# Infini-attention and Hedgehog attention in one kernel: the memory update from f16 halves of the key features, turned by a DMA, and a reordered plan

## The chip, the cores and the metric

The kernel runs on one core of a Trainium2 chip. A core has five engines with an instruction queue each: TensorE (PE in the profile; its weight loads are PEld), VectorE (DVE), ScalarE (ACT), GpSimd (POOL) and SyncE (SP), which here only issues DMAs. The metric is the time of one launch on the device in microseconds, as the median over runs.

## The reference, cut to what matters

Two attention layers on 2048 tokens, width 1024, 32 heads of 32; the results stand side by side in the output.

Part A is attention in four segments of 512 tokens with a memory M and its normaliser z for each head:

```python
phi = lambda t: jnp.where(t > 0, t + 1.0, jnp.exp(t))
for s in range(N):                     # N = 4 segments
    a_dot = softmax(qs @ ks.T * scale + mask) @ vs
    pq = phi(qs)
    num = jnp.einsum("bhld,bhde->bhle", pq, M)
    den = jnp.einsum("bhld,bhd->bhl", pq, z)[..., None] + 1e-6
    outs.append(g * num / den + (1.0 - g) * a_dot)
    pk = phi(ks)
    M = M + jnp.einsum("bhld,bhle->bhde", pk, vs)
    z = z + jnp.einsum("bhld->bhd", pk)
```

Part B is linear attention: per head a feature map (two softmaxes) of a learned projection of queries and keys, sums of key features times values over all tokens, then a quotient for each query. Both parts end in an output product with a 1024 x 1024 matrix.

## The kernel before, in words

**Number format.** Nearly all products take float32 values as two f16 halves (high, and the rest as low) and add three f16 products: high-high, high-low, low-high. ACT makes the high half as a copy with a scale, DVE or POOL the low half by a subtraction. Some products are still in float32; each of those is two records of the trace.

**The plan.** The program records every step as an operation with an engine, an expected duration, a priority and its dependencies (`Graph.op`). `Graph.run` then walks through expected time: whenever an engine is free, it takes the ready operation with the smallest priority (ties by order of recording) and emits it. That fixes the order in every engine's queue, and each queue is worked off in that order. It also hands out the eight PSUM banks by kind ("proj", "s", "misc", "pv", "kv", with limits for each; at most three "proj" at a time). Where it expects PE to wait for more than 0.5 us, `Graph.fill` emits float32 products of an identity matrix with itself into a free bank ("fill"), which keep PE active.

**Part A's units.** A unit is one segment `s` and one group `g` of four heads; 32 units, priority 2u. The first half takes segments 0 and 1 for all groups, the second segments 2 and 3. `produce(u)` projects keys (m = 1), then queries (m = 0), 24 f16 products of 512 columns each, and makes from PSUM the f16 halves of both (`h3`) and the features (`pk` unless the segment is the last, `pq` unless it is the first). SP copies the halves into `st` in the layout that scores need. `values(u)` projects values with 96 products of 128 columns; ACT writes them scaled in float32 to `vf` (three buffers, with a column of ones for each of the four heads). `attend(u)` finds row maxima (L796 products, L802 on DVE), makes the halves `vl` of the values from `vf` (L835 on ACT, L837 on DVE; two buffers), reads the memory (L849), updates it, and does scores (L894), exponential and halves (L898, L900, L901), causal masks on POOL (L907), head products (L930), and writes its result to DRAM.

**The memory update before.** For each of the 24 units whose segment is not the last: `pk` is relu(k) + exp(-relu(-k)), from two Relu steps and an exponential on ACT and an addition on POOL. In `attend`, four float32 transposes on PE turn it (L864), ACT copies the result from PSUM to `pkt` (L626), four float32 products with `vf` give the update (L869), DVE multiplies it with the mask `bdm` (the gate on each head's block, and head columns for z; L872), and POOL adds it to `mem` (L873).

**Around it.** While part A runs, other work is mixed into the queues by priority: loading and splitting of weights and segments; `fold`, which multiplies part B's weights with its feature map; halves of part B's value weights and of two pairs of its token tiles. Then the key stage of part B (`strassen`, feature softmax `expo`, sums L1294 from the halves `pt` of L1284 and L1287), the query stage with the output product of part B (L378 misc), and the output product of part A (L1539). The query stage already turns f16 tiles of 128 x 1024 with a DMA issued by SP (L1467).

**Segment loads.** `load_seg(s)` fetches a segment in two pieces of 1 MB, takes the largest magnitude and makes halves. Segments 0 and 1 have their own slots for both pieces. Segments 2 and 3 share one slot, S11, so the first piece is fetched again after the second was used.

Of the kernel before, what the change touches and what calls it, by code (L numbers as in the profile page):

```python
# [8 lines left out]
F32 = mybir.dt.float32  # L9
# [9 lines left out]
S = 2048  # L19
# [24 lines left out]
EUP = 2.0 ** 15  # L44

# [17 lines left out]
class Op:  # L63
    __slots__ = ("eng", "dur", "fn", "prio", "lat", "deps", "wait", "ready", "short", "port", "banks", "place", "known", "safe", "kb")


class Graph:
# [36 lines left out]
    def op(self, eng, dur, fn, r=(), w=(), prio=0, lat=0.0, short=False, port=False, need=(), kb=256):  # L104
        o = Op()
        o.short, o.port = short, port or eng == "POOL"
        o.eng, o.dur, o.fn, o.prio, o.lat, o.kb = eng, dur, fn, (prio, len(self.ops)), lat, kb
        o.banks = []
        ends, starts = set(), set()
        for b in need:  # L110
            if b.prev[0] is not None:
                ends.update(b.prev[0].ops)
        for write, accs in ((0, r), (1, w)):
            for acc in accs:
                b, key = acc if isinstance(acc, tuple) else (acc, None)
# [24 lines left out]
        self.ops.append(o)  # L140
        return o
# [120 lines left out]
def tile_kernel(ctx: ExitStack, tc: tile.TileContext, ax, aw, awv, awo, beta, bx, bwqk, bwv, bphi, bwo, out):  # L262
# [57 lines left out]
    bdm = ca.tile([128, NG, 132], F32, name="bdm")  # L320
# [6 lines left out]
    vlb = [ca.tile([128, 4, 4, 66], F16, name=f"vl{i}") for i in range(2)]  # L327
# [3 lines left out]
    vfb = [ca.tile([128, 4, 132], F32, name=f"vf{i}") for i in range(3)]  # L331
    for t in vfb:
        nc.gpsimd.memset(t[:, :, 128:132], 1.0)
# [16 lines left out]
    for i in range(NG):  # L350
        op(POOL, 0.3, lambda i=i: nc.gpsimd.tensor_tensor(
            bdm[:, i, 0:128].rearrange("p (h d) -> p h d", d=32), hd[:, :, None].to_broadcast([128, 4, 32]),
            gate[:, 4 * i:4 * i + 4, None].to_broadcast([128, 4, 32]), op=OP.mult), r=[gates], w=[(bdmb, i)], prio=0.3)
        op(DVE, 0.1, lambda i=i: nc.vector.tensor_copy(bdm[:, i, 128:132], hd), w=[(bdmb, i)], prio=0.3)
# [262 lines left out]
    vlb, vfb = ([G.fixed(t) for t in l] for l in (vlb, vfb))  # L617
# [60 lines left out]
    def bounds(k, segs, prio):  # L678


        bd = bds.get(k) or bds.setdefault(k, G.buf("a", [128, 5, 2, 2], F32, "bd", 4))
# [16 lines left out]
        op(POOL, 0.2, lambda: nc.gpsimd.tensor_scalar(bd()[:, 1, v], bd()[:, 0, v], -1.0, None, op0=OP.mult), w=w, prio=prio)  # L698

    def bounds_v(k, segs, prio):  # L700

        bv = bvs.get(k) or bvs.setdefault(k, G.buf("a", [128, 3, 2], F32, "bv", 3))
# [13 lines left out]
        op(POOL, 0.4, lambda: nc.gpsimd.tensor_scalar(bv()[:, 0, v], xsc[:, s0:s0 + n, 0], wvs[:, kk, 0:1], None, op0=OP.mult),  # L716
           r=[*((xscs, x) for x in segs), (wvss, kk)], w=w, prio=prio)

    def values(u):
# [5 lines left out]
        i2, n0, vf = s % 2, 128 * (g % 2), vfb[u % 3]  # L725
# [4 lines left out]
        for j in range(4):  # L730
# [3 lines left out]
        op(ACT, 0.62, lambda: nc.scalar.activation(vf()[:, :, 0:128], ps(), AF.Copy, scale=bv()[:, 0, i2:i2 + 1]),  # L734
           r=[ps, (bv, i2)], w=[vf], prio=P + VPRIO)

    def produce(u):
# [6 lines left out]
        for m in (1, 0):  # L744
# [11 lines left out]
            name = "pk" if m == 1 else "pq"  # L756
            if (m == 1 and s < NSEG - 1) or (m == 0 and s > 0):
                d[name] = p = G.buf("a", [128, 512], F32, name, 2)
# [5 lines left out]
                op(POOL, 1.25, lambda p=p, z=z: nc.gpsimd.tensor_tensor(p(), p(), z(), op=OP.add), r=[z, p], w=[p], prio=E)  # L764
        values(u)

    def attend(u):
        s, g = units[u]
        d, P = un.pop(u), 2 * u + 1
        st, vl, vf, bd, bv, i2 = stk[u % 3], vlb[u % 2], vfb[u % 3], bds[group(u)], d["bv"], s % 2  # L770
# [60 lines left out]

        def v4(t):
            return t()[:, :, 0:128].rearrange("p c (h d) -> p c h d", d=32)

        act(0.52, lambda: nc.scalar.activation(vl()[:, :, :, 33:65], v4(vf), AF.Copy, scale=bv()[:, 2, i2:i2 + 1]),  # L835
            r=[vf, (bv, i2)], w=[(vl, 0)])
        dve(0.6, lambda: nc.vector.scalar_tensor_tensor(  # L837
            vl()[:, :, :, 0:32], v4(vf), bv()[:, 2, i2:i2 + 1], vl()[:, :, :, 33:65], op0=OP.mult, op1=OP.subtract),
            r=[vf, (bv, i2), (vl, 0)], w=[(vl, 1)], port=True)


        amem = None
        if s > 0:
            amem = G.buf("a", [128, 4, 4, 32], F32, "amem", 1)
            for b in range(2):
                ps = bank("misc", [128, 2, 132], "memory")
                for i in range(2):
                    j = 2 * b + i
                    pe(0.237, lambda ps=ps, i=i, j=j: nc.tensor.matmul(  # L849
                        ps()[:, i, :], d["pq"]()[:, 128 * j:128 * j + 128], mem[:, g, :],  # L850
                        start=True, stop=True), r=[d["pq"], (memb, g)], w=[ps], need=[amem])
                dm = G.buf("a", [128, 2, 4], F32, "dm", 2)
                dve(0.1, lambda ps=ps, dm=dm: nc.vector.tensor_scalar(dm(), ps()[:, :, 128:132], 1e-6, None,
# [3 lines left out]
                    amem()[:, 2 * b:2 * b + 2], ps()[:, :, 0:128].rearrange("p c (h d) -> p c h d", d=32),  # L857
                    dm()[:, :, :, None].to_broadcast([128, 2, 4, 32]), op=OP.mult),
                    r=[ps, dm], w=[(amem, b)])
        if s < NSEG - 1:  # L860
            pkt = G.buf("a", [128, 4, 128], F32, "pkt", 1)
            pt_ = bank("misc", [128, 4, 128], "keys")
            for i in range(4):
                pe(0.112, lambda i=i: nc.tensor.transpose(  # L864
                    pt_()[:, i, :], d["pk"]()[:, 128 * i:128 * i + 128], ident), r=[d["pk"]], w=[pt_], need=[pkt])
            act(0.48, copy(pkt, pt_), r=[pt_], w=[pkt])
            pu = bank("misc", [128, 132], "keys")
            for i in range(4):
                pe(0.225, lambda i=i: nc.tensor.matmul(pu(), pkt()[:, i, :], vf()[:, i, :], start=(i == 0),  # L869
                                                      stop=(i == 3)), r=[pkt, vf], w=[pu])  # L870
            mu = G.buf("a", [128, 132], F32, "mu", 1)
            dve(0.2, lambda: nc.vector.tensor_tensor(mu(), pu(), bdm[:, g], op=OP.mult), r=[pu, (bdmb, g)], w=[mu])  # L872
# [369 lines left out]
    for p in range(NT // 2):  # L1242
# [32 lines left out]
        for hb in range(2):  # L1275
            for j in range(2):
                kv = bank("kv", [128, 4, 66], "sums")
                for i in range(2):
# [7 lines left out]
                    sub, ns, d = ((DVE, nc.vector, 0.6) if i else (POOL, nc.gpsimd, 1.28))  # L1286
# [335 lines left out]
```

## Time and profile before

| | |
|---|---|
| median of 3 runs | 1735.99 us (1734.22 to 1736.42) |
| profiled execution, first to last instruction | 1738.3 us |
| PE busy, matmul records | 1696.5 us (98%), 14604 |
| DVE, ACT, POOL busy | 1394.7, 1140.9, 961.8 us |
| mean granted TensorE clock | 0.995 |
| DMA moved | 275.71 MB, mean 159 GB/s |

The profiled execution's own time is its span; no other time is given for it, and it is 2.3 us above the median. In a group of instructions, "out<-in" are the names of the tiles, then stands the count, the busy time in us, the mean duration in ns, and the idle time of the engine just before them with what ended it. PE's instructions overlap, so busy time divided by the count is smaller than the mean duration. Stretches are counted from the first instruction.

### The profile page before, as it was taken

To read this page: it belongs to the slowest core of one execution; us is meant where nothing else is said; L and a number is where in the kernel's file an instruction comes from. 1 tells how busy PE (TensorE), PEld (TensorE's weight loads), DVE (VectorE), ACT (ScalarE), POOL (GpSimd) and SP (SyncE) were. 2 spreads that over 40 slices of the span, in tenths; PEclk is the share of its full clock that TensorE was granted. 3 is DMA by queue.
4 is the path that set the end of the run, shared out by engine and by line. 5 is a ranking of instruction groups with operands and counts; after the bars stand their busy time and mean duration, and the time that the engine had idled before them with its cause. 6 is when DMAs were issued, how large, how long until landed. Compare 5 with 4: busy or idle time off the path is not lost. (4 is left out here: it accounts for less than half of the span.)

```text
span 1738.3 us, 38775 instructions
## 1 busy us (share of the span) xinstructions
PE 1696.5 (98%) x14604; PEld 1027.0 (59%) x14604; DVE 1394.7 (80%) x3197; ACT 1140.9 (66%) x2083; POOL 961.8 (55%) x1301
## 2 busy tenths in 40 slices
PE   8999999999999999999999999999999999999998
PEld 6767767667776767766754444444544444454443
DVE  6989889789878878788885999996998777696441
ACT  6987887888778776878765767654664554454331
POOL 6446354445757775867755545453588898541000
PEclk9999999999999999999999999999999999999999
DMA  6546545457544643565466443346555774576311
GB/s 203 192 133 173 154 143 177 146 163 233 153 148 136 150 130 113 161 209 149 128 202 241 141 164 128 128 164 233 217 146 146 172 193 134 128 206 171 110 65 61
DMA packets 240844, 275.71 MB, mean 159 GB/s; under 512 B 137488, under 2 KB 190480, under 8 KB 231952
## 3 DMA queue, kind: packets, MB, share of 16 engines
q1 hardware_dynamic: 240656, 273.22, 51.8%
q8 instruction: 115, 1.88, 0.5%
q14 instruction: 73, 0.60, 0.1%
HBM read 145.44 MB, written 85.00 MB: 133 GB/s over the span
## 5 line engine op out<-in xcount | busy, mean ns | idle before, releaser
L378 PE MATMUL proj<-S,S 128*128 128x512 f16 (+1 forms) x3072 | 499.8, 300 | 2.8 <-ACT S L405 0.7
L378 PEld LDWEIGHTS <-S 128*128 128x128 f16 x4608 | 330.6, 98 | 150.5 <-issue 5.5
L574 PE MATMUL proj<-S,S 128*128 128x512 f16 x1488 | 345.4, 380 | 9.2 <-ACT cs L580 4.9
L574 PEld LDWEIGHTS <-S 128*128 128x128 f16 x1968 | 187.0, 98 | 224.9 <-issue 10.4
L907 POOL TENSOR_SCALAR_AFFINE_SELECT ph<-ph 128x256 f16<-128x256 f16 (+1 forms) x448 | 193.5, 453 | 167.3 <-DVE ph L901 148.1
L901 DVE SCALAR_TENSOR_TENSOR ph<-s,ph 128x512 f16<-128x512 f32 x320 | 210.3, 684 | 66.1 <-ACT ph L900 64.0
L802 DVE CUSTOM_DVE_ANT_0 s<-s,causal 128x256 f32<-128x256 f32 (+3 forms) x512 | 242.5, 509 | 16.5 <-PE s L796 13.2
L898 ACT ACTIVATE s<-s,bd 128x512 f32<-128x512 f32 x320 | 211.8, 705 | 25.1 <-PE s L894 23.1
L900 ACT ACTIVATE ph<-s 128x512 f16<-128x512 f32 x320 | 189.3, 651 | 0.9
L378 PE MATMUL misc<-S,ot 128*128 128x512 f16 x768 | 170.7, 379 | 0.0
L1147 ACT ACTIVATE e<-e,sk 128x256 f32<-128x256 f32 x256 | 114.5, 498 | 84.8 <-DVE e L1144 81.1
L378 PEld LDWEIGHTS <-ot 128*128 128x128 f16 x768 | 73.7, 98 | 87.6
L796 PE MATMUL s<-S 96*128 96x512 f16 (+3 forms) x512 | 113.3, 299 | 3.1 <-DVE mt L802 1.5
L894 PE MATMUL s<-S 104*128 104x512 f16 (+3 forms) x512 | 113.8, 299 | 1.1 <-DVE mt L802 0.9
L1444 POOL TENSOR_TENSOR e<-e,zb 128x512 f32<-128x512 f32 x64 | 84.9, 1340 | 44.9 <-DVE r L1150 38.8
L378 PE MATMUL proj<-wv,S 128*128 128x128 f16 x1536 | 107.9, 220 | 1.0 <-DVE mt L802 0.7
L930 PEld LDWEIGHTS <-ph 128*128 128x128 f16 x2560 | 87.4, 96 | 16.6 <-issue 1.8
L930 PE MATMUL pv<-vl,ph 128*128 128x66 f16 (+1 forms) x2560 | 92.6, 184 | 1.9 <-POOL ph L907 0.8
L1150 DVE TENSOR_REDUCE r<-e 128x32 f32<-128x1024 f32 x64 | 76.7, 1203 | 15.9 <-ACT e L1147 15.8
L574 PE MATMUL s<-S,S 128*128 128x512 f16 x324 | 77.4, 379 | 0.0
L1287 POOL TENSOR_TENSOR pt<-e,pt 128x512 f16<-128x512 f32 x32 | 38.6, 1209 | 65.9 <-ACT pt L1284 63.2
L802 DVE DVE_READ_ACCUMULATOR2_ANT mt<- 128x1 f32 x512 | 71.8, 140 | 0.0
(330 smaller groups left out, 3313.1 us busy)
## 6 DMA issues: line engine op xcount, KB each, us to landing
S<-h SPq DMA_DIRECT2D x192, 128.0 KB
S<-wf_d SPq DMA_DIRECT2D x21, 1024.0 KB
st<-bwqk SPq DMA_DIRECT2D x64, 256.0 KB
wf_d<-fo SPq DMA_DIRECT2D x48, 256.0 KB
out<-os SPq DMA_DIRECT2D x39, 256.0 KB
wf_d<-oT SPq DMA_DIRECT2D x36, 256.0 KB
S<-xf_d SPq DMA_DIRECT2D x9, 1024.0 KB
S<-aw SPq DMA_DIRECT2D x16, 512.0 KB
```

Source lines behind the costliest of these rows:

```text
L378: op(PE, dur, lambda c=c, a=a, b=b, lv=lv, rv=rv: nc.tensor.matmul(pv(), lv(), rv(), start=(c == 0 and a + b == 0), stop=(c == n - 1 and a ...
L574: op(PE, 0.215, lambda n=n, a=a, b=b, lv=lv, rv=rv: nc.tensor.matmul(ps(), lv(), rv(), start=(start and n == 0 and a + b == 0), stop=(n == ...
L796: nc.tensor.matmul(ps()[:, o:o + 128 * i + 128], st()[0:96, 0, h, 128 * i:128 * i + 128], st()[0:96, 1, h, 0:128 * i + 128], start=True, s ...
L802: dve(0.12 + 0.00113 * n, lambda h=h, i=i, o=o, n=n: nc.vector.tensor_tensor_reduce(ps()[:, o:o + n], ps()[:, o:o + n], causal[:, 512 - n: ...
L894: nc.tensor.matmul(ps()[:, o:o + n], st()[0:104, 1, h, 128 * j:128 * j + 128], st()[0:104, 0, h, 128 * j:512], start=True, stop=True)
L898: act(0.59, lambda: nc.scalar.activation(ps(), ps(), AF.Exp, bias=0.0, scale=bd()[:, 4, i2, 0:1]), r=[(bd, i2)], w=[ps])
L900: act(0.5, lambda: nc.scalar.activation(ph()[:, 0], ps(), AF.Copy, scale=2.0 ** 14), r=[ps], w=[(ph, 0)])
L901: dve(0.6, lambda: nc.vector.scalar_tensor_tensor(ph()[:, 1], ps(), 2.0 ** 14, ph()[:, 0], op0=OP.mult, op1=OP.subtract), r=[ps, (ph, 0)], ...
L907: nc.gpsimd.affine_select(pd, pd, pattern=[[0, n], [1, 128]], compare_op=OP.is_ge, fill=0.0, base=0, channel_multiplier=-1)
L930: nc.tensor.matmul(ps()[:, i, n0:n1], ph()[:, a, o:o + 128], vl()[:, j, h, n0:n1], start=(i == 0 and a == 0), stop=(j == min(i, 2)), skip_ ...
L1147: op(ACT, 0.41, lambda i=i: nc.scalar.activation(e()[:, 4 * i:4 * i + 4], e()[:, 4 * i:4 * i + 4], AF.Exp, bias=0.0, scale=sk()[:, i:i + 1 ...
L1444: op(POOL, 1.35, lambda a=a, h0=h0, e=e: nc.gpsimd.tensor_tensor(e()[:, 8 * a:8 * a + 8], e()[:, 8 * a:8 * a + 8], zv()[:, h0:h0 + 8], op= ...
```

## The change

- **Key features.** `pk` is made scaled so that it fits f16: ACT takes relu(k) with one scale (`bd` row 6) and exp(k) straight from PSUM; POOL takes min(exp, 1) times a scale and adds the Relu; ACT makes the high half and POOL the low half (`pkh`, one buffer).
- **Turning.** One DMA per unit, issued by SP, turns both halves together (128 x 1024 f16) into `pkt` (one buffer). The transposes on PE and the copy from PSUM go.
- **Update.** Twelve f16 products of 132 columns into one bank, with the value halves `vl` as moving operand. The mask becomes `bdu`, which carries the scales (two small steps on POOL per unit). Columns of ones now stand after each head's 32 values, so `mem` and the readers of L849's result use that layout.
- **Values.** `vf` goes. ACT makes the high half and DVE the low half from PSUM with the combined scale (`bv` row 3); `vl` has three buffers.
- **Bounds.** A few small operations per set of bounds make the scales above.
- **Third segment.** Segment 2 gets the slots of segment 3 for its two pieces (S6 and S7) and is fetched once.
- **Plan.** Every operation's priority gets an offset of at most 0.3, 0.7, 1.5 or 3.0, fixed by a table of numbers for 40 of the stretches of 60 operations; consecutive PE operations of one kind share an offset.
- **Low halves of the last two pairs in the key stage** (p = 6, 7): all on POOL instead of half on DVE.

In the built programs this makes on PE 288 weight loads and products `vl,pkt` for 96 transposes and 96 update products, and 32 fillers for 74; on SP 24 more transposes and one load fewer; on POOL 130 more instructions, on ACT 56 fewer, on DVE 28 more.

```diff
+STRETCH, REACH = 60, (0.3, 0.7, 1.5, 3.0)
+NUDGE = {0: 465887, 3: 912202, 5: 876263, 7: 730503, 8: 455190, 9: 72936, 13: 804475, 14: 476942, 15: 772345, 18: 258321,
...
+def nudge(at):
+    seed = NUDGE.get(at // STRETCH, 0)
+    if not seed:
+        return 0.0
...
+    return REACH[seed & 3] * (2 * (x / 4294967296.0) - 1)
...
+        o.base, o.at = prio, len(self.ops)
+        last = self.ops[-1] if self.ops else o
+        if o.eng == "PE" and (last.eng, last.base, last.fn.__code__, last.banks) == (o.eng, prio, fn.__code__, o.banks):
+            o.at = last.at
+        o.prio = (prio + nudge(o.at), len(self.ops))
...
-               lambda i: G.buf("slot", [128, 4, 512], F32, f"S{4 + 2 * s + i // 4}" if first else "S11"), 4, 1 if first else 4,
-               half4(t), (xscs, s, lambda: xsc[:, s]), prio, sub=sub, keep=first, line="segments", dep=dep,
+               lambda i: G.buf("slot", [128, 4, 512], F32, f"S{4 + 2 * min(s, 1) + i // 4}" if s < NSEG - 1 else "S11"), 4, 1 if first else 4,
+               half4(t), (xscs, s, lambda: xsc[:, s]), prio, sub=sub, keep=s < NSEG - 1, line="segments", dep=dep,
...
+        op(DVE, 0.1, lambda: nc.vector.tensor_scalar(
+            bd()[:, 5, v, 0], bd()[:, 3, v, 1], 0.25, 2.0 ** -14, op0=OP.mult, op1=OP.add), w=w, prio=prio)
+        op(DVE, 0.12, lambda: nc.vector.reciprocal(bd()[:, 5, v, 1], bd()[:, 5, v, 0]), w=w, prio=prio)
+        op(POOL, 0.2, lambda: nc.gpsimd.tensor_tensor(bd()[:, 6, v, 0], bd()[:, 0, v, 1], bd()[:, 5, v, 1], op=OP.mult), w=w, prio=prio)
...
-        op(ACT, 0.62, lambda: nc.scalar.activation(vf()[:, :, 0:128], ps(), AF.Copy, scale=bv()[:, 0, i2:i2 + 1]),
-           r=[ps, (bv, i2)], w=[vf], prio=P + VPRIO)
+        op(ACT, 0.62, lambda: nc.scalar.activation(vl()[:, :, :, 33:65], v4(), AF.Copy, scale=bv()[:, 3, i2:i2 + 1]),
+           r=[ps, (bv, i2)], w=[(vl, 0)], prio=P + VPRIO)
+        op(DVE, 0.8, lambda: nc.vector.scalar_tensor_tensor(
+            vl()[:, :, :, 0:32], v4(), bv()[:, 3, i2:i2 + 1], vl()[:, :, :, 33:65], op0=OP.mult, op1=OP.subtract),
+            r=[ps, (bv, i2), (vl, 0)], w=[(vl, 1)], prio=P + VPRIO)
...
+            if m == 1 and s < NSEG - 1:
+                p, ph = G.buf("a", [128, 512], F32, "pk", 2), G.buf("a", [128, 2, 512], F16, "pkh", 1)
+                z = G.buf("a", [128, 512], F32, "z", 1)
+                op(ACT, 0.59, lambda z=z, ps=ps: nc.scalar.activation(z(), ps(), AF.Relu, scale=bd()[:, 6, i2, 0:1]),
+                   r=[ps, (bd, i2)], w=[z], prio=E)
+                op(ACT, 0.59, lambda p=p, ps=ps: nc.scalar.activation(p(), ps(), AF.Exp, bias=0.0, scale=bd()[:, 0, i2, 1:2]),
+                   r=[ps, (bd, i2)], w=[p], prio=E)
+                op(POOL, 1.57, lambda p=p: nc.gpsimd.tensor_scalar(
+                    p(), p(), 1.0, bd()[:, 5, i2, 1:2], op0=OP.min, op1=OP.mult), r=[(bd, i2)], w=[p], prio=E)
+                op(POOL, 1.25, lambda p=p, z=z: nc.gpsimd.tensor_tensor(p(), p(), z(), op=OP.add), r=[z], w=[p], prio=E)
+                op(ACT, 0.53, lambda p=p, ph=ph: nc.scalar.activation(ph()[:, 0], p(), AF.Copy), r=[p], w=[(ph, 0)], prio=E)
+                op(POOL, 1.28, lambda p=p, ph=ph: nc.gpsimd.tensor_tensor(ph()[:, 1], p(), ph()[:, 0], op=OP.subtract),
+                   r=[p, (ph, 0)], w=[(ph, 1)], prio=E)
+                d["pkt"] = pkt = G.buf("a", [128, 2, 4, 128], F16, "pkt", 1)
+                op(SP, 0.6, lambda ph=ph, pkt=pkt: nc.sync.dma_start_transpose(
+                    pkt().rearrange("p a j f -> p (a j) f"), ph().rearrange("p a t -> p (a t)")),
+                   r=[(ph, 0), (ph, 1)], w=[pkt], prio=E, lat=2.0, kb=512)
...
-        act(0.52, lambda: nc.scalar.activation(vl()[:, :, :, 33:65], v4(vf), AF.Copy, scale=bv()[:, 2, i2:i2 + 1]),
-            r=[vf, (bv, i2)], w=[(vl, 0)])
-        dve(0.6, lambda: nc.vector.scalar_tensor_tensor(
-            vl()[:, :, :, 0:32], v4(vf), bv()[:, 2, i2:i2 + 1], vl()[:, :, :, 33:65], op0=OP.mult, op1=OP.subtract),
-            r=[vf, (bv, i2), (vl, 0)], w=[(vl, 1)], port=True)
...
-            pt_ = bank("misc", [128, 4, 128], "keys")
-            for i in range(4):
-                pe(0.112, lambda i=i: nc.tensor.transpose(
-                    pt_()[:, i, :], d["pk"]()[:, 128 * i:128 * i + 128], ident), r=[d["pk"]], w=[pt_], need=[pkt])
-            act(0.48, copy(pkt, pt_), r=[pt_], w=[pkt])
...
-                pe(0.225, lambda i=i: nc.tensor.matmul(pu(), pkt()[:, i, :], vf()[:, i, :], start=(i == 0),
-                                                      stop=(i == 3)), r=[pkt, vf], w=[pu])
+                for i in range(4):
+                    for a, o in ((0, 33), (0, 0), (1, 33)):
+                        nc.tensor.matmul(pu(), pkt()[:, a, i, :], vl()[:, i, :, o:o + 33], start=(i == 0 and a == 0 and o == 33),
+                                         stop=(i == 3 and a == 1))
...
-            load_seg(2 + u // 4, 2 * u + 2.5, DVE)
+            load_seg(2 if u == 3 else 3, 2 * u + 2.5, DVE)
...
-                    sub, ns, d = ((DVE, nc.vector, 0.6) if i else (POOL, nc.gpsimd, 1.28))
+                    sub, ns, d = ((DVE, nc.vector, 0.6) if i and p < VT[0] else (POOL, nc.gpsimd, 1.28))
```

More of the change, by code (lines that the diff above doesn't have):

```diff
@@ L63 @@
 class Op:
-    __slots__ = ("eng", "dur", "fn", "prio", "lat", "deps", "wait", "ready", "short", "port", "banks", "place", "known", "safe", "kb")
+    __slots__ = ("eng", "dur", "fn", "prio", "lat", "deps", "wait", "ready", "short", "port", "banks", "place", "known", "safe", "kb", "at", "base")
+def nudge(at):
+    seed = NUDGE.get(at // STRETCH, 0)
+    if not seed:
+        return 0.0
+    x = (at * 2654435761 & 0xFFFFFFFF) ^ (seed * 2246822519 + 374761393 & 0xFFFFFFFF)
+    x ^= x >> 15
+    x = x * 2246822519 & 0xFFFFFFFF
+    x ^= x >> 13
+    x = x * 3266489917 & 0xFFFFFFFF
+    x ^= x >> 16
+    return REACH[seed & 3] * (2 * (x / 4294967296.0) - 1)
 class Graph:
@@ L326, in tile_kernel @@
     nc.gpsimd.memset(mem, 0.0)
-    vlb = [ca.tile([128, 4, 4, 66], F16, name=f"vl{i}") for i in range(2)]
+    vlb = [ca.tile([128, 4, 4, 66], F16, name=f"vl{i}") for i in range(3)]
     for t in vlb:
@@ L616, in tile_kernel @@
            w=[(t, (1, 3))], prio=0.3)
-    vlb, vfb = ([G.fixed(t) for t in l] for l in (vlb, vfb))
+    vlb = [G.fixed(t) for t in vlb]
     memb = G.fixed(mem)
@@ L860, in attend, with f @@
         if s < NSEG - 1:
-            pkt = G.buf("a", [128, 4, 128], F32, "pkt", 1)
-            pt_ = bank("misc", [128, 4, 128], "keys")
-            for i in range(4):
-                pe(0.112, lambda i=i: nc.tensor.transpose(
-                    pt_()[:, i, :], d["pk"]()[:, 128 * i:128 * i + 128], ident), r=[d["pk"]], w=[pt_], need=[pkt])
-            act(0.48, copy(pkt, pt_), r=[pt_], w=[pkt])
-            pu = bank("misc", [128, 132], "keys")
-            for i in range(4):
-                pe(0.225, lambda i=i: nc.tensor.matmul(pu(), pkt()[:, i, :], vf()[:, i, :], start=(i == 0),
-                                                      stop=(i == 3)), r=[pkt, vf], w=[pu])
-            mu = G.buf("a", [128, 132], F32, "mu", 1)
-            dve(0.2, lambda: nc.vector.tensor_tensor(mu(), pu(), bdm[:, g], op=OP.mult), r=[pu, (bdmb, g)], w=[mu])
+            pkt, bdu = d["pkt"], d["bdu"]
+            mu = G.buf("a", [128, 132], F32, "mu", 1)
+            pu = bank("misc", [128, 4, 33], "keys")
+            def f():
+                for i in range(4):
+                    for a, o in ((0, 33), (0, 0), (1, 33)):
+                        nc.tensor.matmul(pu(), pkt()[:, a, i, :], vl()[:, i, :, o:o + 33], start=(i == 0 and a == 0 and o == 33),
+                                         stop=(i == 3 and a == 1))
+            pe(0.7, f, r=[pkt, vl], w=[pu], need=[mu])
+            dve(0.2, lambda: nc.vector.tensor_tensor(
+                mu(), pu().rearrange("p h d -> p (h d)"), bdu().rearrange("p h d -> p (h d)"), op=OP.mult), r=[pu, bdu], w=[mu])
             pool(0.43, lambda: nc.gpsimd.tensor_tensor(mem[:, g, :], mem[:, g, :], mu(), op=OP.add),
```

43 lines of the change are left out of this document (25 added, 18 removed), and 4 rows, old and new, of the table NUDGE.

## The prediction

> **What bounds the kernel now.** I read the page first: busy shares, and the granted clock by slices.
>
> ```profile
> span 1738.3 us, 38775 instructions
> PE 1696.5 (98%) x14604; PEld 1027.0 (59%) x14604; DVE 1394.7 (80%) x3197; ACT 1140.9 (66%) x2083; POOL 961.8 (55%) x1301
> PEclk9999999999999999999999999999999999999999
> ```
>
> TensorE is busy nearly all the span at an almost full clock. An average hides stages, so next came the busy time of each engine by stretch: load-up, attention (30 to 840), its end and hand-over, keys of part B, then queries and the output products. Columns are the stretch, its length, and busy time of PE, PEld, DVE, ACT and POOL.
>
> ```profile
> 0.00:30.00 30.00, 25.15 (x148) 19.97 (x148) 21.08 (x56) 23.04 (x31) 16.55 (x28) 0.94 0.63 215
> 30.00:840.00 810.00, 798.98 (x8693) 568.50 (x8694) 692.88 (x2004) 640.73 (x1164) 488.13 (x774) 1.00 0.54 159
> 840.00:960.00 120.00, 114.57 (x925) 68.74 (x922) 90.12 (x214) 74.16 (x131) 69.74 (x97) 0.97 0.62 202
> 960.00:1290.00 330.00, 317.21 (x2202) 162.38 (x2201) 299.34 (x505) 208.66 (x428) 171.75 (x166) 1.00 0.48 166
> 1290.00:1739.00 449.00, 440.55 (x2649) 207.38 (x2647) 291.23 (x423) 194.29 (x330) 215.62 (x239) 1.00 0.50 138
> ```
>
> In attention PE idles 11.0 of 810 us (810 - 798.98); VectorE (DVE) has 693, ScalarE (ACT) 641, GpSimd (POOL) 488. So there PE work removed should come off the time nearly one for one, as long as DVE, at 86%, can keep up. From 840 to 1290 PE idles 18.2 us (5.4 + 12.8), with DVE at 91% in the key stage.
>
> Then PE's groups by shape: those that go (transposes L864, update L869, fillers L336) and the nearest rows to those that come.
>
> ```profile
> L864 PE MATMUL misc<-ident,pk 128*128 128x128 f32 x96 | 16.1, 281 | 2.6 <-DVE mt L802 2.6
> L869 PE MATMUL misc<-vf,pkt 128*128 128x132 f32 x192 | 28.5, 281 | 0.1
> L336 PE MATMUL fill<-ident 128*128 128x128 f32 x148 | 23.6, 305 | 0.0
> L378 PE MATMUL proj<-wv,S 128*128 128x128 f16 x1536 | 107.9, 220 | 1.0 <-DVE mt L802 0.7 <-DVE ph L901 0.2
> L1475 PE MATMUL pv<-pt,st 128*64 128x128 f16 x768 | 27.4, 221 | 0.1
> L378 PEld LDWEIGHTS <-S 128*128 128x128 f16 x4608 | 330.6, 98 | 150.5 <-issue 5.5
> ```
>
> Matmuls overlap, so the price of one is busy time over count, not its mean: 107.9 / 1536 = 70 ns for a 128-column f16 product, against 16.1 / 96 = 168 ns for a float32 transpose and 28.5 / 96 = 297 ns for a float32 update product (two records each).
>
> **PE's memory update.** It runs in the 24 of 32 units whose segment is not the last. Gone: 96 transposes and 96 float32 products, 16.1 + 28.5 = 44.6 us. Come: 12 f16 products per unit, 288, each with a 128-column weight load and 132 columns. By the f16 row of the same shape 70 x 132/128 = 72 ns, so 20.8 us. Bounds: the cheapest f16 row, 27.4 / 768 = 36 ns, gives 10.3; weight loads that hide behind nothing, 98 ns, give 28.2. I take 20.8, the row of the same shape: net -23.8, between -34.3 and -16.4.
>
> The Trainium skill ("TensorE: Matmul & The Clock Gate", section "Back-to-back issue gap") gives about 81 ns for each pair of weight load and 128-column matmul in a sustained stream. By that 288 cost 23.3 us and the net is an estimate of -21.3; the trace has 70 ns for the pair here, so the page's figure is somewhat dear, and the sum doesn't use it.
>
> **Fillers.** The planner puts dummy float32 products where it expects PE to wait over 0.5 us. In the order of the built programs 74 become 32 (each two of the 148 records). The first 11 stay; 20 between 840 and 960 become 10, 29 around 1200 to 1290 become 5, 14 later become 6.
>
> ```profile
> 1283.85 2.05 PE L336 MATMUL fill<-ident 128*128 128x128 f32 x16
> 1286.74 1.60 PE L336 MATMUL fill<-ident 128*128 128x128 f32 x12
> ```
>
> At this hand-over from keys to queries, two filler bursts separate head products. In the new order 24 query products stand there instead, and key-sum blocks that stood back to back have such products between them. So real work is in the gaps. 84 records x 23.6 / 148 = 159 ns: -13.4 us. If the gaps stay, 0; if the other idle time of 840 to 1290 goes too, up to 18.2 more.
>
> **ACT.** Groups that go (L734 writes the float32 values, kept here as the f16 half):
>
> ```profile
> L734 ACT ACTIVATE vf<-proj,bv 128x512 f32<-128x512 f32 x32 | 23.4, 730 | 26.9 <-PE proj L378 26.6
> L835 ACT ACTIVATE vl<-vf,bv 128x512 f16<-128x512 f32 x32 | 25.4, 795 | 3.6 <-PE pv L930 3.3
> L763 ACT ACTIVATE pk<-pk 128x512 f32<-128x512 f32 x24 | 16.2, 677 | 0.2
> L626 ACT ACTIVATE pkt<-misc 128x512 f32<-128x512 f32 x24 | 15.6, 652 | 1.0 <-PE misc L864 1.0
> ```
>
> L835, L763 and L626 vanish, 57.2 us; the new f16 copy of the key features costs 24 x 0.652 = 15.6. The exponential takes the place of a Relu with one form. Net -41.6, not on PE's path: worth 0 directly.
>
> **DVE.** The low half of the values now reads PSUM.
>
> ```profile
> L837 DVE SCALAR_TENSOR_TENSOR vl<-vf,bv,vl 128x512 f16<-128x512 f32 x32 | 30.2, 948 | 0.2
> L750 DVE SCALAR_TENSOR_TENSOR h<-proj,bd,h 128x512 f16<-128x512 f32 x64 | 47.6, 744 | 9.5 <-ACT h L748 5.7 <-ACT z L761 2.3 <-ACT pk L761 1.1
> L692 DVE SCALAR_TENSOR_TENSOR bd<-bd 128x2 f32<-128x2 f32 x14 | 4.9, 351 | 0.0
> ```
>
> 32 x (948 - 744) = -6.5 us; two small bounds operations in 18 sets at most at L692's price, 36 x 0.351 = +12.6, at least 0. Between -6.5 and +6.1, taken as 0. A product's PSUM bank is now held until DVE has read it too, a 744 ns step plus its turn: the third "proj" bank covers that; without cover 32 x 0.74 = 24 us.
>
> **POOL and SP.** The nearest rows:
>
> ```profile
> L1070 POOL TENSOR_SCALAR S<-S,wsc 128x512 f32<-128x512 f32 x16 | 25.6, 1601 | 1.7 <-DMA S<-bwv 1.5 <-DVE bd L689 0.2
> L485 POOL TENSOR_TENSOR fo<-quad,fo 128x512 f16<-128x512 f32 x32 | 38.1, 1191 | 10.9 <-ACT fo L484 10.8
> L351 POOL TENSOR_TENSOR bdm<-hd,gate 128x128 f32<-128x128 f32 x8 | 2.9, 398 | 0.0
> L694 POOL TENSOR_TENSOR bd<-xsc,wgs 128x4 f32<-128x4 f32 x14 | 3.3, 234 | 3.6 <-DVE bd L689 2.1 <-DVE wgs L391 1.6
> POOL ph L907 <- DVE ph L901: 133.6, 122, 4.2
> L1467 SPq DMA_TRANSPOSE pt<-kls x64: 1232/1258/4816, 1273.6 to 1579.4; - x64
> L754 SPq DMA_DIRECT2D S<-h x192: 547/572/1697, 31.6 to 868.5; - x192
> PE pv L930 <- POOL ph L907: 0.8, 3, 0.4
> PE proj L378 <- DVE mt L802: 0.7, 2, 0.5
> ```
>
> Per unit POOL gains the scaling 1.60, the low half 1.19, the scaled mask 0.40 and its four columns 0.23: 3.42, in 24 units 82 us, and 27 small bounds operations 6 us: +88 in attention, of 322 idle there (810 - 488), 133.6 of it waiting for DVE before a mask (the fifth row, of 30 to 840). Direct price 0. But masks L907 stand behind these on POOL's in-order queue, the head products L930 behind the masks, and six "ph" buffers are the cover.
>
> SP gains 24 transposes at 1.26 us, 30 us. Each waits for POOL's low half, and with one "pkt" buffer for PE's preceding update; the copies of the next unit's query halves (L754) are queued behind it, and those feed scores a unit later; units follow each other every (868.5 - 31.6) / 31 = 27 us by that row. Cover: those 27 us; price without it, 1.26 to 4.8 us a unit (median and longest transpose).
>
> For both I enlarge PE's 11.0 us of idle time in attention by POOL's growth, 88 / 488 = 18%: +2.0. Bounds: -2.6 (the wait of transpose L864 goes with it) and 24 x 1.19 = 28.6, a low half's length per unit.
>
> Third segment: one 1 MB load fewer of some 276 MB, DMA share 0.54: 0. The eight low halves that move from DVE to POOL take 8 x 0.865 = 6.9 us from DVE where it is at 91%, and give POOL (52%) 8 x 1.209 = 9.7: 0, inside the idle bound above.
>
> ```profile
> L1287 DVE TENSOR_TENSOR pt<-e,pt 128x512 f16<-128x512 f32 x32 | 27.4, 865 | 4.7 <-ACT pt L1284 4.6
> L1287 POOL TENSOR_TENSOR pt<-e,pt 128x512 f16<-128x512 f32 x32 | 38.6, 1209 | 65.9 <-ACT pt L1284 63.2 <-DVE mx L1140 2.7
> ```
>
> **Sum.** -23.8 - 13.4 + 2.0 = -35.2. The profiled span of 1738.3 becomes 1703.1. The median of the three runs is 2.3 lower (1735.99), so 1701.
>
> **Rivals.**
> 1. The gaps remain: fillers go, PE idles as long. 1701 + 13.4 = 1714. For it: the fillers were put where a producer was late. Against: the new order has real products there.
> 2. The gaps close as well: half to all of the 18.2 us of idle time, 1692 to 1683. For it: the key stage's waits are for single ACT and DVE results that another order can pass. Against: DVE is at 91% there.
> 3. DVE becomes the bound of attention, and only the fillers' part is gained: 1736 - 13 = 1723. POOL's growth lengthens DVE's operations with two SBUF inputs, as L837's mean of 948 against 744 suggests. Against: the longest such group, L837, leaves SBUF; what remains grows by 18% of a few microseconds.
> The Trainium skill ("SBUF — State Buffer", section "SBUF: two separate sides") says that a DVE operation with two SBUF inputs and a GpSimd operation that reads SBUF exclude each other for a whole instruction. By that rule more POOL work speaks against the change, and the new source of the low half for it; L837 beside L750 agrees with it.
> 4. Slower: POOL's chain delays masks, so head products and then PE wait. The gain is 37.2 us without the new waits, so it decides from 37.2 / 24 = 1.6 us a unit, one POOL scaling before an urgent mask. With scaling and low half both in the way, 24 x 2.8 = 67: 1736 - 37 + 67 = 1766. For it: POOL is in order. Against: PE's waits for masks are 0.8 us now, and POOL waits 133.6 us for DVE before them.
>
> **Numbers.** Likeliest 0.44 (1701, own range 1690 to 1711), rival 1 0.20, rival 2 0.18, rival 3 0.07, rival 4 0.11. The range 1683 to 1726 leaves out rival 4 and the edges. About 0.2%, 3.5 us, is what a measurement can tell: faster 0.86, same 0.03 (rival 3 or 4 stopping near zero), slower 0.11.
>
> **What would show it.** Right: the update's products near 70 ns of busy time each, PE busy about 1659 us (1696.5 - 23.8 - 13.4), attention some 22 us shorter, POOL busier by about 90. Wrong: PE waiting for POOL's masks or DVE's maxima tens of microseconds in attention (rivals 3 and 4), waits for transposes, or idle time in place of the fillers (rival 1). The price of the update's products and the new waits are the weakest terms.

## The result and the profile after

The changed kernel takes 1704.01 us (median of 4 runs, 1701.91 to 1707.45) against 1735.58 us (1734.22 to 1736.42) of the kernel before: a ratio of 0.9820, 95% interval 0.9806 to 0.9834. The time forecast was 1701. The profiled execution has a span of 1702.8 us and a time of 1704.9, 2.1 above it. In all runs with both numbers the time is 1.7 to 2.4 us above the span. By that the profiled execution of the kernel before, with its span of 1738.3, took about 1740 (an estimate), over 4 us more than the median. So differences of the two profiles, such as the 35.5 us below, are some 4 us larger than those of the medians, 31.6.

First the page of the changed kernel, span and busy times:

```profile
span 1702.8 us, 38814 instructions
PE 1669.9 (98%) x14520; PEld 1001.0 (59%) x14520; DVE 1399.3 (82%) x3225; ACT 1113.4 (65%) x2027; POOL 1072.7 (63%) x1431
```

The span is 35.5 us shorter; 26.6 of it is PE's busy time (1696.5 to 1669.9), 8.9 its idle time (41.8 to 32.9). POOL has 110.9 us more work. The changed kernel's groups by shape, those that the prediction priced:

```profile
L918 PE MATMUL misc<-vl,pkt 128*128 128x132 f16 x288 | 21.1, 221 | 0.0
L358 PE MATMUL fill<-ident 128*128 128x128 f32 x64 | 10.1, 298 | 0.0
L805 POOL TENSOR_SCALAR pk<-pk,bd 128x512 f32<-128x512 f32 x24 | 49.6, 2067 | 15.2 <-ACT pk L803 15.2
L809 POOL TENSOR_TENSOR pkh<-pk,pkh 128x512 f16<-128x512 f32 x24 | 27.8, 1156 | 2.1 <-ACT pkh L808 1.9
L817 POOL TENSOR_SCALAR bdu<-bdm,bv,bd 128x128 f32<-128x128 f32 x24 | 13.4, 559 | 0.2 <-DVE mu L922 0.2
L820 POOL TENSOR_SCALAR bdu<-bdm,bd 128x4 f32<-128x4 f32 x24 | 7.2, 299 | 0.0
L767 DVE SCALAR_TENSOR_TENSOR vl<-proj,bv,vl 128x512 f16<-128x512 f32 x32 | 23.6, 738 | 2.3 <-ACT vl L765 2.2
L400 PE MATMUL proj<-S,S 128*128 128x128 f16 x1536 | 108.1, 220 | 0.1
```

The last of these groups before:

```profile
L378 PE MATMUL proj<-S,S 128*128 128x128 f16 x1536 | 102.4, 219 | 0.6 <-ACT oT L626 0.6
```

The update's products cost 21.1 / 288 = 73 ns each. So the update takes 23.5 us less of PE (44.6 to 21.1) and the fillers 13.5 less (23.6 to 10.1), 37.0 together. PE's busy time falls by only 26.6. Of the 10.4 us between, 6.2 are the net growth of the other groups, with this last one growing most (102.4 to 108.1): all groups of PE together fell by 30.8 (2169.4 to 2138.6). The other 4.2 are overlap: matmuls of different groups overlap, so before the groups added up to 2169.4 us where PE was busy 1696.5, and what is taken from a group need not come off PE's busy time in full.

To see where the time went, both spans are cut at events of the program, not at fixed times: the first key sum of part B, the last one, the last head product of part B's queries, the end. The first two come from the rows of the key sums, before and then after:

```profile
L1294 PE MATMUL kv<-ot,pt x768: 189/192/204, 967.0 to 1251.8; 128*128 128x65 f16 x128, 128*128 128x64 f16 x64
```

```profile
L1345 PE MATMUL kv<-ot,pt x768: 189/192/262, 942.3 to 1224.5; 128*128 128x65 f16 x128, 128*128 128x64 f16 x64
```

Stretches of the kernel before by these marks (columns as in the prediction: stretch, length, busy time of PE, PEld, DVE, ACT, POOL, then granted clock, DMA share, GB/s):

```profile
0.00:967.00 967.00, 945.70 (x9791) 660.50 (x9792) 810.64 (x2282) 743.90 (x1338) 578.98 (x901) 0.99 0.55 165
967.00:1251.80 284.80, 274.71 (x1943) 139.66 (x1942) 255.89 (x428) 178.25 (x368) 139.22 (x129) 1.00 0.49 174
1251.80:1586.40 334.60, 329.38 (x2198) 160.49 (x2196) 265.31 (x397) 167.84 (x302) 243.59 (x273) 1.00 0.61 157
1586.40:1738.30 151.90, 146.68 (x688) 66.32 (x682) 62.82 (x93) 50.88 (x78) 0.00 (x0) 1.00 0.26 96
```

and of the changed kernel:

```profile
0.00:942.30 942.30, 924.40 (x9765) 639.94 (x9765) 818.00 (x2312) 713.48 (x1279) 681.89 (x1023) 0.99 0.63 175
942.30:1224.50 282.20, 273.41 (x1926) 138.78 (x1925) 251.59 (x425) 178.15 (x367) 148.64 (x137) 0.99 0.48 173
1224.50:1551.20 326.70, 324.34 (x2155) 155.51 (x2151) 263.68 (x393) 170.26 (x304) 242.16 (x273) 1.00 0.63 162
1551.20:1702.80 151.60, 147.71 (x691) 66.76 (x685) 66.03 (x98) 51.52 (x79) 0.00 (x0) 1.00 0.26 97
```

Attention with its hand-over is 24.7 us shorter (PE busy 21.3 less, idle 3.4 less), the key stage 2.6, the query stage 7.9, the end 0.3. PE's own list of waits after the change holds nothing large:

```profile
PE misc L880 <- DVE mh L875: 3.8, 3, 2.5
PE s L854 <- DVE ph L952: 2.5, 3, 2.1
PE kv L1345 <- POOL pt L1338: 1.5, 3, 0.7
PE pv L981 <- POOL ph L958: 0.5, 2, 0.3
```

Most of this looks as forecast. The theory to be tested: the 23.5 us of PE work come off the time by themselves, the order removes the fillers, and POOL's work is hidden. The main rival: the order earns the gain, and the other steps alone are worth little or less than nothing. The kernel before was timed again beside each group of runs, with medians from 1735.2 to 1737.9 us; every ratio is to the one beside it, and times of different groups can be compared to about 3 us only.

### The profile page after: what moved, and what is told of

It reads as the page before. It is cut to its first block, busy times and chain, and to the rows that moved or that the text cites. A ratio compares the mean times of both kernels' runs of the same rounds, so it can differ in the third digit from the quotient of the medians.

```text
span 1702.8 us, 38814 instructions
## 1 busy us (share of the span) xinstructions
PE 1669.9 (98%) x14520; PEld 1001.0 (59%) x14520; DVE 1399.3 (82%) x3225; ACT 1113.4 (65%) x2027; POOL 1072.7 (63%) x1431
## 4 chain that ended last, share of the span: by engine, by line
PE 59%; DVE 13%; ACT 3%; issue 1%; DMA 1%; POOL 1%; SPq 0%; ACTq 0%; DVEq 0%; POOLq 0%
PE proj L400 14%; PE proj L596 11%; PE misc L400 10%; PE proj L1590 5%; PE s L1590 2%; PE s L945 2%; PE s L854 2%; PE pv L981 2%; DVE mx L1191 2%; PE s L596 2%; DVE r L1201 1%; PE pv L1526 1%; DVE S L429 1%; PE misc L1590 1%; PE misc L596 1%
## 5 line engine op out<-in xcount | busy, mean ns | idle before, releaser
L400 PE MATMUL proj<-S,S 128*128 128x128 f16 (+1 forms) x3072 | 503.3, 300 | 2.1 <-ACT S L427 0.7
L860 DVE CUSTOM_DVE_ANT_0 s<-s,causal 128x256 f32<-128x256 f32 (+3 forms) x512 | 241.9, 511 | 13.3 <-PE s L854 10.4
L949 ACT ACTIVATE s<-s,bd 128x512 f32<-128x512 f32 x320 | 211.0, 706 | 47.7 <-PE s L945 46.6
L1338 POOL TENSOR_TENSOR pt<-e,pt 128x512 f16<-128x512 f32 x40 | 50.1, 1264 | 49.2 <-ACT pt L1335 49.2
```

Source lines behind the costliest of these rows:

```text
L400: op(PE, dur, lambda c=c, a=a, b=b, lv=lv, rv=rv: nc.tensor.matmul(pv(), lv(), rv(), start=(c == 0 and a + b == 0), stop=(c == n - 1 and a ...
L860: dve(0.12 + 0.00113 * n, lambda h=h, i=i, o=o, n=n: nc.vector.tensor_tensor_reduce(ps()[:, o:o + n], ps()[:, o:o + n], causal[:, 512 - n: ...
L949: act(0.59, lambda: nc.scalar.activation(ps(), ps(), AF.Exp, bias=0.0, scale=bd()[:, 4, i2, 0:1]), r=[(bd, i2)], w=[ps])
```

## The experiments

### The order: the table taken away, exchanged, shortened, and given to the kernel before

No offsets, all other parts of the change kept:

```diff
-NUDGE = {0: 465887, 3: 912202, ...
+NUDGE = {}
```

> The changed kernel with an empty table of offsets, so the planner's own order; 93 fillers. By my sum the update is worth 23.8 us and the order 13.4: if so, 1704 + 13 = 1717, with the key update products unchanged at about 21 us of PE. By the rival that the order carries little, 1704 to 1708; by the rival that the update alone gains nothing without the new order, 1730 or more.

Measured: 1741.17 us, ratio to the kernel before 1.0036 (1.0023 to 1.0049). Without the offsets the change makes the kernel slower, and the table is worth 37 us, not 13. The page, the update's group and the stretches by the same marks:

```profile
span 1742.6 us, 39030 instructions
PE 1695.1 (97%) x14642; PEld 1018.9 (58%) x14642; DVE 1403.0 (81%) x3225; ACT 1108.2 (64%) x2027; POOL 1075.4 (62%) x1431
```

```profile
L914 PE MATMUL misc<-vl,pkt 128*128 128x132 f16 x288 | 21.1, 222 | 0.2 <-DVE ph L948 0.2
L354 PE MATMUL fill<-ident 128*128 128x128 f32 x186 | 29.2, 302 | 0.0
```

```profile
0.00:967.30 967.30, 939.83 (x9823) 650.48 (x9824) 821.41 (x2318) 710.31 (x1282) 676.19 (x1023) 0.99 0.58 170
967.30:1256.40 289.10, 280.16 (x1975) 144.01 (x1974) 254.49 (x420) 178.59 (x369) 151.99 (x137) 0.99 0.48 171
1256.40:1595.20 338.80, 331.62 (x2187) 159.65 (x2184) 265.38 (x398) 169.81 (x302) 247.18 (x273) 0.99 0.61 159
1595.20:1742.60 147.40, 143.47 (x673) 64.80 (x667) 61.70 (x91) 49.51 (x76) 0.00 (x0) 1.00 0.25 91
```

The update is as cheap as in the changed kernel (21.1 us), yet the first key sum comes at 967.3, where it came before the change (967.0). Up to there PE is busy 5.9 us less and idle 6.2 more (27.5 against 21.3). Fillers take 6.2 us more there (17.8 against 11.6), so a part of what the update saved went into gaps and fillers. Against the changed kernel the span is 39.8 longer: 19.1 of fillers, 14.6 of idle time, and 6.1 of other busy time. The clock may explain the last: the mean granted clock is 0.990 against 0.994; the part of full speed that is missing, times the span, is 17.4 us of lost clock against 10.2 (an estimate).

Other offsets with the same largest sizes in the same stretches:

```diff
     if not seed:
         return 0.0
+    seed += 4
```

> The changed kernel with the same stretches and reaches but other random offsets (105 fillers). If any shaking of the order does as well, 1704 within 5 us; if the particular order in the table is what closes the gaps, as I think, 1715 to 1725, like the kernel with an empty table or worse.

Measured: 1747.38 us, ratio 1.0070 (1.0055 to 1.0085): slower than with none. So it isn't enough to shake the order; that is shown for this one other draw.

The table for the first part of the recorded operations only (stretches 0 to 27, and 0 to 177):

```diff
-NUDGE = {0: 465887, ... 27: 417957, 166: 472397, ... 177: 212495, 207: 30091, ... 258: 979208}
+NUDGE = {0: 465887, ... 27: 417957}
...
+NUDGE = {0: 465887, ... 177: 212495}
```

> The changed kernel with the offsets of stretches 0 to 27 alone: PE's order equals that of the changed kernel for the first 60% of its instructions, into the end of attention, then goes its own way (82 fillers). If the loss of the kernel without offsets (1741) lies in the load-up and attention, 1715 to 1720, with part B's stages as long as without offsets; if it lies in the hand-overs and part B, 1735 to 1741.

> The changed kernel with the offsets of stretches 0 to 177: PE's order equals the changed kernel's for the first 74% of its instructions, into the key stage of part B (54 fillers). With offsets to 27 alone the time was 1731.6, with all 1704.0. If the hand-over from attention to the key stage is where the later offsets gain, 1712 to 1718; if the hand-over from keys to queries and the query stage, 1725 to 1731.

Measured: 1731.57 us (0.9964, 0.9954 to 0.9974) and 1709.19 us (0.9853, 0.9838 to 0.9868). Step by step: none 1741.2, the first group of offsets 1731.6, the second 1709.2, the third 1704.0. Stretches to the first and the last key sum, with offsets 0 to 27:

```profile
0.00:950.80 950.80, 927.53 (x9794) 643.07 (x9795) 812.35 (x2313) 709.72 (x1275) 679.16 (x1022) 0.99 0.62 173
950.80:1246.30 295.50, 282.30 (x1982) 144.32 (x1981) 260.15 (x426) 182.62 (x377) 150.18 (x137) 0.99 0.47 167
```

and with 0 to 177:

```profile
0.00:942.40 942.40, 923.60 (x9763) 639.58 (x9764) 817.12 (x2312) 712.99 (x1279) 682.17 (x1023) 0.99 0.63 175
942.40:1226.40 284.00, 276.36 (x1957) 141.16 (x1956) 255.35 (x430) 179.29 (x371) 150.89 (x138) 1.00 0.48 174
```

The first group brings the first key sum forward by 16.5 us (967.3 to 950.8) but lengthens the key stage (289.1 to 295.5). The second brings it forward by 8.4 more and takes 11.5 from the key stage: of the table's 37 us, 22 come with this second group, most of them (8.4 + 11.5) in the hand-over from attention to keys and in the keys themselves. The third leaves the first key sum where it is (942.3) and gains behind it.

The same table in the kernel before:

```diff
+STRETCH, REACH = 60, (0.3, 0.7, 1.5, 3.0)
+NUDGE = {0: 465887, 3: 912202, ...
...
+        o.prio = (prio + nudge(o.at), len(self.ops))
```

> The kernel before with the same table of offsets on its own operations, update unchanged (74 fillers). If the table is fitted to the changed kernel's operations, it is a random shake here: 1735 to 1748, as other offsets did on the changed kernel (1747). If a reordering of this kind gains by itself, 1715 to 1725.

Measured: 1743.01 us, ratio 1.0050 (1.0033 to 1.0068). The stretches are counted in recorded operations, and those are others here. So this table alone makes the kernel before slower, and the rest of the change alone makes it slower; both together are faster. What an order made for the kernel before would be worth isn't shown by this.

### Fillers

```diff
-    G.filler = lambda ps: nc.tensor.matmul(ps, ident, ident, start=True, stop=True)
+    G.filler = None
```

In the kernel before:

> The kernel before without its 74 fillers; order of everything else unchanged. If the fillers stand in gaps that PE would have waited through anyway (my theory: the new plan gained by having fewer gaps), PE's idle time grows by about what the fillers took (23.6 us busy) and the time stays at 1736 within 5 us, or grows where the clock drops. If the fillers themselves were the cost (rival: the change gained by dropping them), the time falls by 13 to 19 us, to 1717 to 1723.

In the changed kernel:

> The changed kernel without its 32 fillers; all else unchanged. Theory (they stand in gaps): 1704 within 4 us. Rival (they are the cost): 10.1 us busy, of which 4.2 in the first 60 us, so 1704 - 6 = 1698 or less.

Measured: 1742.44 us (1.0038, 1.0025 to 1.0050) and 1706.59 us (0.9835, 0.9820 to 0.9849). Fillers aren't a cost that can be saved. Without them the kernel before is 6.7 us slower, and its clock is lower. (The changed kernel is 2.6 slower, which the intervals don't tell from nothing.) The profiled execution without fillers:

```profile
core 0: 1738.6 us, clock 0.992
```

Its clock of 0.992 against 0.995 in the profile before is about 5 us of lost clock; the medians over the runs, 0.991 without fillers and 0.996 for the kernel before beside them, give about 9 (estimates as above). A fall in fillers is a sign that the planner sees fewer gaps, and no gain by itself.

### PE work added and taken away

The changed kernel with its twelve update products run twice (each pass starts the sum anew):

```diff
-                for i in range(4):
+                for i in (0, 1, 2, 3, 0, 1, 2, 3):
```

> The changed kernel with its order kept, the twelve update products emitted twice (the second set starts the sum anew). The second set costs the 21.1 us of the first if PE bounds attention: 1725. If PE had slack: 1704 to 1712.

The changed kernel with eight more float32 products per update, about the PE time of the old update:

```diff
+                for i in range(8):
+                    nc.tensor.matmul(pu(), ident, bdm[:, g], start=True, stop=True)
```

> The changed kernel with its order kept, and in each update eight float32 products of 128 and 132 columns put before the twelve f16 ones: PE gets back about the 44.6 us (8 x 24 float32 products at 0.30 us, 57 us at most) of work that the change removed, nothing else changes. If PE's work counts one for one when the order stands still, 1704 + 45 to 57, so 1749 to 1761. If attention has slack that the order alone made use of, 1725 or less.

The kernel before with one float32 product per update instead of four:

```diff
-                pe(0.225, lambda i=i: nc.tensor.matmul(pu(), pkt()[:, i, :], vf()[:, i, :], start=(i == 0),
-                                                      stop=(i == 3)), r=[pkt, vf], w=[pu])
+                pe(0.225, lambda i=i: nc.tensor.matmul(pu(), pkt()[:, i, :], vf()[:, i, :], start=True, stop=True)
+                   if i == 3 else None, r=[pkt, vf], w=[pu])
```

> The kernel before with its order kept and three of the four float32 update products of each unit left out (the memory is then wrong): 72 x 0.297 = 21.4 us of PE work less, nearly the 23.5 that the change saved. If the saving is real in a fixed order, 1736 - 21 = 1715. If the order of before can't use it (DVE or ACT decide in attention), 1728 to 1736.

Measured: 1722.77 us (0.9917, 0.9902 to 0.9931), 1747.99 us (1.0061, 1.0044 to 1.0078), and 1729.57 us (0.9954, 0.9939 to 0.9968). The groups that were changed, in that order:

```profile
L918 PE MATMUL misc<-vl,pkt 128*128 128x132 f16 x576 | 38.4, 221 | 0.0
```

```profile
L917 PE MATMUL misc<-bdm,ident 128*128 128x132 f32 x384 | 47.7, 278 | 0.0
```

```profile
L869 PE MATMUL misc<-vf,pkt 128*128 128x132 f32 x48 | 9.8, 287 | 0.0
```

In the changed kernel, adding costs nearly one for one: 17.3 us more of the group lengthen the span by 17.2 (1702.8 to 1720.0), and 47.7 lengthen it by 45.1 (to 1747.9); by the ratios to the kernel before it is 17 and 42. In the kernel before, taking away doesn't pay one for one: 18.7 us less of the group (28.5 to 9.8) shorten it by 8.3 (1737.86 to 1729.57), 44%. Adding in the kernel before and taking away in the changed one weren't tried. The stretch of this kernel up to the first key sum shows the rest:

```profile
0.00:959.40 959.40, 928.69 (x9647) 639.93 (x9648) 810.20 (x2282) 743.19 (x1338) 578.73 (x901) 0.99 0.55 166
```

PE is busy 17.0 us less there but idle 9.4 more (30.7 against 21.3): in an order laid out for the longer work, what comes next isn't ready yet. By the price of adding, the changed kernel with only the 23.5 us of the update's saving put back would take 1725 to 1727 us (an estimate, not run). In this order, then, nearly all of the update's saving is earned, and 9 to 11 us come from the rest. An order made for the longer update could be better than that.

### POOL and the turning DMA

Two more scalings by 1.0 on POOL for each update:

```diff
...
+                    nc.gpsimd.tensor_scalar(p(), p(), 1.0, bd()[:, 5, i2, 1:2], op0=OP.min, op1=OP.mult)
+                    for _ in range(2):
+                        nc.gpsimd.tensor_scalar(p(), p(), one[:, 0:1], None, op0=OP.mult)
...
```

> The changed kernel in its order, with two more scalings by 1.0 of the key features on POOL in each of the 24 updates: 24 x 2 x 1.6 to 2.07 = 77 to 99 us more POOL work in front of masks, as much again as the change brought. If POOL has the slack I said, 1704 to 1710. If POOL's chain is on PE's path (rival 4, decided from 1.6 us a unit), 24 x 3.2 = 77 more, 1760 to 1780; anything near 1730 says that the added POOL work of the change itself costs some of the gain.

Each turning DMA issued twice, the second after the first has landed:

```diff
...
+                    for _ in range(2):
+                        nc.sync.dma_start_transpose(pkt().rearrange("p a j f -> p (a j) f"), ph().rearrange("p a t -> p (a t)"))
...
```

> The changed kernel in its order, with each turning DMA issued twice; SP waits for the first to land before it issues the second, so each unit's SP queue is held by some 1.4 us of issue and the landing, 3 to 5 us in all. If the copies queued behind have the slack I said (27 us), 1704 to 1708; if SP's queue is on the path of the scores, 24 x 3 = 72 more.

Measured: 1768.62 us (1.0193, 1.0165 to 1.0221) and 1718.28 us (0.9904, 0.9889 to 0.9919). The added group, the first stretch, the chain of work that ended last by engine, and PE's waits for POOL, all of the kernel with more POOL work:

```profile
L808 POOL TENSOR_SCALAR pk<-pk,one 128x512 f32<-128x512 f32 x48 | 75.8, 1579 | 4.6
```

```profile
0.00:1005.40 1005.40, 944.01 (x9764) 650.37 (x9765) 826.89 (x2312) 712.19 (x1279) 759.34 (x1071) 0.97 0.57 164
```

```profile
PE 60%; DVE 19%; POOL 9%; ACT 6%; issue 3%; DMA 2%; SPq 0%; DVEq 0%; ACTq 0%; POOLq 0%
```

```profile
PE pv L985 <- POOL ph L962: 11.0, 11, 2.4
PE misc L903 <- POOL pq L797: 5.8, 1, 5.8
PE misc L1017 <- POOL osum L1012: 4.6, 4, 3.4
```

75.8 us of work on an engine that is busy 63% of the span lengthen the span by 63.0 us (1765.8 against 1702.8), and all of that lies before the first key sum (1005.4 against 942.3). PE idles 61.4 us there instead of 17.9. By the three rows 21.4 of it are waits for POOL itself (0.5 in the changed kernel): 11.0 for masks L962, as rival 4 had it, 5.8 at once for the features of a unit's queries, and 4.6 for osum, a unit's result. The rest are waits for other engines, and that these are POOL's delays passed on is likely, since nothing else was changed. PE is also busy 19.6 us longer there, with the same instructions. The same line of the chain in the changed kernel:

```profile
PE 59%; DVE 13%; ACT 3%; issue 1%; DMA 1%; POOL 1%; SPq 0%; ACTq 0%; DVEq 0%; POOLq 0%
```

POOL's share of the chain rises from 1% to 9%. The mean granted clock falls from 0.994 to 0.985, which is some 16 us more of lost clock (an estimate as above).

The second DMA is a smaller case of the same. Its rows:

```profile
L814 SPq DMA_TRANSPOSE pkt<-pkh x48: 1232/1280/3108, 51.0 to 834.0; - x48
SPq L814 <- DMA pkt<-pkh: 72.5, 24, 6.2
```

```profile
0.00:955.80 955.80, 927.90 (x9765) 640.82 (x9766) 817.17 (x2312) 712.42 (x1279) 681.73 (x1023) 0.99 0.64 179
```

24 more issues at 1.28 us are 30.7 us of SP's queue, and before them SP waits 72.5 us for the first DMA to land (second row: total, times, longest). So SP is held 103 us more, 4.3 a unit; the span grows by 13.9, 0.6 us a unit, and 13.5 of it before the first key sum, mostly as idle time of PE (27.9 against 17.9).

## Why the prediction was right, and where it was not

**PE's update (-23.8): size right, reading wrong.** The group fell by 23.5, at 73 ns a product instead of 72. The Trainium skill ("TensorE: Matmul & The Clock Gate", section "Back-to-back issue gap") gives about 81 ns for a pair with 128 columns; the trace has 73 for 132. (A group's busy time overlaps its neighbours', so PE's own busy time may have fallen by less.) But the step that made it time, that PE work removed in attention "should come off the time nearly one for one", failed. It was read from 11 us of idle time in 810. With the update replaced and no offsets, the first key sum comes 0.3 us later than before; with work simply left out, 44% came through. Here little idle time went with adding that costs. It didn't say that removing would pay: that depends on whether the next step can come sooner.

**Fillers (-13.4): right in size (13.5), and right that the gaps don't stay as idle time.** PE's idle time after the first key sum fell too, from 20.5 to 15.0 us, a part of rival 2. The kernels without fillers show that the gain isn't the saved products themselves; that real work now stands in the gaps fits the smaller idle time.

**The order as a term.** It was given 13.4 us of 35.2, by its fillers. It is worth 37 us in the changed kernel, 25 of them up to the first key sum (967.3 to 942.3), where the prediction had given it 3 (20 of the 84 records) and the update nearly all. The terms aren't independent: with the planner's own order the update's saving isn't earned at all, and this change brings both.

**POOL's "direct price 0": it held, but not for the reason given.** The new order leaves PE's waits for masks at 0.5 us, so rival 4 doesn't show in the changed kernel. The reason given, the 133.6 us in which POOL waited before masks, is an average and no cover: with 75.8 us more of POOL work in the same order 63.0 us, 0.83 of it, came onto the time. How much less would already cost isn't shown. POOL's growth was also undersized: 102.9 us up to the first key sum (578.98 to 681.89) instead of 88, mainly the scaling L805 at 2067 ns instead of 1601 and the mask L817 with L820 at 858 instead of 632. Whether this growth ate the update's gain in the kernel without offsets is open. PE's direct waits don't say so: up to the first key sum PE waits 1.2 us for POOL there, against 0.8 in the kernel before. POOL's work wasn't taken out by itself.

**The new waits (+2.0): wrong sign.** PE's idle time fell by 8.9; yet 10.4 us of PE's busy time stayed for which there was no term, 6.2 in other groups and 4.2 by overlap. What lengthens those groups is open; the clock (0.994 against 0.995) gives 1.5 of it, as an estimate. That -8.9 and +10.4 add up to +1.5, near the +2.0 of the sum, is luck.

**SP's 27 us of cover: for the most part.** With SP held 4.3 us more a unit by the doubled DMA, 0.6 us a unit came onto the time: less than one transpose (1.26), not nothing.

**DVE 0: nearly.** Up to the first key sum it grew by 7.4 us, 1.3 above the upper bound. The low half from PSUM took 738 ns against the 948 of the one from SBUF, 6 from the row it was priced by. The Trainium skill ("SBUF — State Buffer", section "SBUF: two separate sides") says that a DVE operation with two SBUF inputs and a GpSimd operation that reads SBUF exclude each other; that fits, though no run here separates it from the other source by itself. Rival 3 didn't come: DVE is busy 87% up to the first key sum (818.0 of 942.3), and PE waits little for it.

**The sum as a whole.** The forecast span of 1703.1 us is near the measured 1702.8. The time was 3 us off because 2.3 us were taken off the span to come to a median; that was the distance of one execution of the kernel before, which by its estimated time of 1740 us was a long one. The size came out right, but the shares did not: what was put down to the update alone needed the order, and the terms that were left out happened to cancel.

**Still open.** How much of the 5.5 us that the kernel without offsets loses is the new work on POOL and SP, and how much the luck of one planned order against another (other offsets moved it by 6 us, the table moved the kernel before by 8). An order searched for the kernel before wasn't tried; it would be the fair counterpart. The values' halves from PSUM, the third segment's slots and the low halves of the last two pairs weren't tried alone.

## What to carry to other kernels

In a kernel whose queues are laid out by a plan, test a change once with the old way of ordering: here the new order was worth more (37 us) than the work removed (23.5), and without it the removal didn't pay. PE's busy share of 98% told what added work would cost, and not what removed work would bring; doubling a suspect and removing it are different questions. POOL's slack, summed over a stage, was no cover: before pricing work on such an engine at nothing, add as much again and see.

## What the runs showed of the hardware

Dummy products on PE were worth having in one of the two kernels: leaving 148 records out cost 6.7 us in the kernel before and lowered the granted clock from 0.996 to 0.991 (medians over the runs). In the changed kernel 64 records made no difference that can be told (2.6 us). The kernel with the most waiting (more POOL work) was granted 0.985. A POOL scaling of 128 x 512 float32 with two operations, a minimum and a multiplication by a value from a tile, took 2067 ns; the same shape with the multiplication alone took 1579.
